# Attention with few key-value heads and an MLP: row maxima by pairs, with a difference product on ScalarE

## The chip, the cores and the metric

The kernel runs on one core of a Trainium2 chip. The metric is the device time of one execution in microseconds, the median of several runs; lower is better. The engines are PE (TensorE: products), ACT (ScalarE), DVE (VectorE), POOL (GpSimd) and SP (SyncE, which issues the transfers). Sums of products go to PSUM, in eight banks of 128 x 512 numbers; ScalarE and VectorE read them there.

## The reference

The computation is one transformer block on x (1 x 2048 x 512) with 32 query heads of 16 numbers each, all on one head of keys and values, and an MLP of 1376 hidden numbers. Six vectors from c and w_mod shift, scale and gate the two halves.

```python
h = _layernorm(x, axis=-1) * (1 + ca) + sa
q = (h @ wq).reshape(B, S, H, Dh)          # 32 heads of 16
k = h @ wk                                 # one head
v = h @ wv
scores = jnp.einsum("bhqd,bkd->bhqk", q, k) * (Dh ** -0.5)
p = softmax(scores); o = p @ v
x = x + ga * (o @ wo)
h = _layernorm(x, axis=-1) * (1 + cb) + sb
x = x + gb * (gelu(h @ w1 + b1) @ w2 + b2)
```

The softmax subtracts each row's maximum over all 2048 keys. That maximum is what the change is about: it takes one product of queries with keys only to find it, and a second one for the scores that are exponentiated.

## The kernel before, in words

Numbers are kept at fp32 accuracy by splitting operands into a high and a low part (`split`, L128), so that most products come in threes.

**Prologue** (L1241 to L1302, some 75 us): the first normalization, keys (`ks`, L109: 64 rows for each half of the array), values (`va`), and the first queries. Tiles that only the prologue needs are in the pool `pro`.

**Main loop** (L1350 to L1448). The queries are cut into 8 blocks of 256 rows, a block into 8 units of 4 heads: 64 units. A unit runs in 4 passes of the loop, a pass in two *half cycles*. A half cycle issues, in an order that `issue` (L1320) and `mixture` (L1330) write out from lists:

- four maximum products `m` (`Max.step`, L498 to L506): 128 queries by 512 keys, each on one half of the array (s = 0 or 1). Each goes to one of three banks (tag "m"), and VectorE reduces it to a column of `mx` (L510). The list of a side (L488) goes along the four key blocks kc of a row of queries. When a unit's list is through, `put_max` (L529) joins the columns and writes the maxima into the queries' tile, so that the score product subtracts them.
- four score products `e` of a later unit (`sexp`, L590 to L607) into three banks in turn (L586), each followed by the exponential on ScalarE into a tile p (L611). There are three p tiles of four slots.
- a batch of *filling products* of other work, where the queue has one (`take`, L1169): late query projections (qps, L448), output projection (wops, L864), turns of the normalized rows (tp, L928), the MLP's two matrices (w1ps, L990, and w2ps, L1022). The two sides of the array take half of each.
- at its end 16 products `acc` of p and values for an earlier step (`pv`, L617 to L628, each of two passes, of which the trace has one record each).

Each engine has its own queue and takes it in the order in which the program issues (L214). In the loop there are three forms of half cycles. `short` (L1395) is a batch of at most four products' worth of 512 columns: six with 256 columns at the start of w1ps, three left over at the start of w2ps, four turns, four late query products. Their order is (first half; the second has the sides exchanged):

```python
issue(mixture(maxes(1, n // 2), exps(1, [(X, 0), (X, 1)])),
      exps(0, [(X, 0)]) + halves(batch, 0) + [(1.0, lambda: follow(0, X, 1))])
```

Larger batches have an order of their own (L1400 and L1430). Without a batch, `plain` (L1381) takes two maximum products of each side, and one of them gets the bank "x" as its fourth. `issue` takes from the list that has got less far, the first list on a tie.

Behind the loop the last block's rest runs by itself ("fast", L821 to L825 load its weight pieces into the free p tiles). A queue of jobs (`put_off`, L1166) decides which filling work comes when; clocks (`later`, L145) count half steps, not time. Copies out of PSUM in that work are on ScalarE at L454 (late queries in small batches) and L895 (turned rows).

Of the kernel before, what the change touches and what calls it, by code (L numbers as in the profile page):

```python
# [18 lines left out]

GELU_R = 0.044715 ** 0.5  # L20

LEAD = 6
# [23 lines left out]
def raw(ap):  # L46
    return ap.bitcast(F32)
# [3 lines left out]
def adaln_mqa_mlp(  # L51
# [199 lines left out]
    load_x(1)  # L251
    nc.sync.dma_start(out=wqf[:, :, P:2 * P], in_=wqr[:, :, P:2 * P])
    load_x(2)
    nc.sync.dma_start(out=wqf[:, :, 2 * P:D], in_=wqr[:, :, 2 * P:D])
    load_x(3)
    qbufs = [att.tile([P, 2, HQ], F32R, name=f"qst{i}") for i in range(QBUFS)]

    qbufs = [att.tile([P, 2, HQ], F32R, name=f"qst{i}") for i in range(QBUFS)]
# [47 lines left out]

    pad(pro, 64, "pad2")
    wkH = pro.tile([P, KD, P], F32R, name="wkH")
# [171 lines left out]
    class Max:  # L480


        def __init__(self):
            def products(u, kcs):
                return [(u, j, t, kc) for kc in kcs for j in range(2) for t in range(blocks[units[u][0]][1] // P)]

            def in_rows(u):
                return [(u, j, t, kc) for j in range(2) for t in range(blocks[units[u][0]][1] // P) for kc in range(NKC)]  # L488


            begin = [o for u, kc in FIRST_MAX for o in products(u, [kc])]
            self.todo = [begin + [o for u in range(2, NU) for o in in_rows(u)] for _ in range(2)]
            self.mx, self.left, self.done = {}, list(size), 0

        def has(self, s):
            return bool(self.todo[s])

        def step(self, s, hold=None, **place):  # L498
            u, j, t, kc = self.todo[s].pop(0)
            T = blocks[units[u][0]][1] // P  # L500
            if u not in self.mx:
                self.mx[u] = att.tile([P, 4 * T, NKC], F32, name=f"mx{u}", tag="mx", bufs=2)
            m = psum.tile([P, 512], F32, name=f"m{u}_{j}_{t}_{kc}_{s}", **(place or dict(tag="m", bufs=3)))
            rows = slice(64 * s, 64 * s + 64)
            nc.tensor.matmul(m, qsts[u][rows, j, t * P:(t + 1) * P], ks[rows, kc * 512:(kc + 1) * 512],  # L505
                             start=True, stop=True)  # L506
            i = (s * 2 + j) * T + t

            def reduce():
                nc.vector.tensor_reduce(out=self.mx[u][:, i, kc:kc + 1], in_=m, axis=AX.X, op=ALU.max)  # L510
                self.left[u] -= 1
                if self.left[u] == size[u] // 2 and u > 1 and u + 1 < NU:
                    load_q(u + 1)
                if self.left[u] == 0:
# [14 lines left out]
    def put_max(u, mx):  # L529
# [36 lines left out]
        else:  # L566
            later((0 - clock[0]) % 4 + 1, reduce)

    pbufs = {}
    ocs = []  # L570
# [19 lines left out]
    def sexp(u, K, j, s, line=None):  # L590

        w = blocks[units[u][0]][1]
        qst = qsts[u]
        assert u in placed
        n = u * steps[0] + K
        if n < 3 and n not in pbufs:
            pbufs[n] = att.tile([P, 2, 2, 512], F32, name=f"p{n}", tag="p", bufs=3)
        pt = pbufs[n % 3]
# [4 lines left out]
        if w == 512:  # L603
            kt, rhs = K, qst[rows, j, :]
        else:
            kt, rhs = 2 * K + j, qst[rows].rearrange("p j n -> p (j n)")
        nc.tensor.matmul(e, ks[rows, kt * P:(kt + 1) * P], rhs, start=True, stop=True)  # L607
        dst = pt[:, j, s, :]

        def exp():  # L610
            ins = nc.scalar.activation(dst, e, AF.Exp, scale=0.25)  # L611
            for old in written.pop((n - 3, j, s), ()):
                tc.declare_no_dep(ins.ins, old, reason="the products that read the tile's last contents come between the two")
            written.setdefault((n, j, s), []).append(ins.ins.name)
            return ins

        return exp() if line is None else line.append(exp)  # L617

    def pv(u, K):
        w = blocks[units[u][0]][1]  # L620
        if K == 0:
            accs[u] = psum.tile([P, w], F32, name=f"acc{u}", tag="v")
        pt = pbufs[(u * steps[0] + K) % 3]
        for kt in ([K] if w == 512 else [2 * K, 2 * K + 1]):
            for cidx in range(4):
                s, j = divmod(cidx, 2)
                rhs = pt[:, j, s, :] if w == 512 else pt[:, kt - 2 * K, s, j * w:(j + 1) * w]
                ins = nc.tensor.matmul(accs[u][32 * cidx:32 * cidx + 32, :], va[:, kt, :], rhs,  # L628
                                       start=kt == 0, stop=kt == NKT - 1)
                if kt % 2 and cidx:  # L630
                    wait_early(ins)

    def finish_unit(u):
# [174 lines left out]
    def rest_steps(b, fast, rp, bank, ons, ready):  # L808
# [4 lines left out]
        for hf in range(w // HQ):  # L813
# [7 lines left out]
            if fast:  # L821
                for f in range(3, 9, 2):
                    two = att.tile([P, 2, 2, KD, P], F32R, name=f"w1t{b}_{hf}_{f}", tag="p", bufs=3)
# [68 lines left out]
            def modulate(dp, ps):  # L892
                if not fast:
                    src = rp.tile([P, 2, HQ], F32, name=f"tc{b}_{hf}_{dp}", tag="ot", bufs=2)
                    nc.scalar.copy(src, ps)  # L895
                for d2 in range(2):
# [453 lines left out]
    for u in range(NU):  # L1350
        for K in range(0, steps[u], 2):
# [59 lines left out]
            if batch:  # L1411
# [88 lines left out]
```

## Time and profile before

| | before |
|---|---|
| time of the runs, median of three | 1564.88 us (1564.7 to 1564.99) |
| span of the profiled execution, first to last instruction | 1563.1 us |
| VectorE: maximum reduces | 2048, mean 682 ns |
| ScalarE: exponentials | 2048, mean 598 ns |
| granted TensorE clock | 1.000 |

The profiled execution has no time of its own in the record beside its span; the runs' median is 1.8 us above it. In the profile's lines, `L510 DVE TENSOR_REDUCE mx<-m ... x2048 | 1270.5, 682` means: line 510, on VectorE, writes mx from m, 2048 times, 1270.5 us in which at least one was under way, 682 ns each on average; then the idle time before them and what ended it. Neighbours overlap, so that the time from one start to the next is shorter than the duration. In the view in order of time a row is start, duration, engine, line, operation, tiles and count; neighbours of one form are merged.

### The profile page before, as it was taken

Reading aid. Unit: us, or ns where it says so; the run is one execution under the profiler, and the core shown is the slowest. Engines: PE = TensorE matmul, PEld = TensorE weight load, DVE = VectorE, ACT = ScalarE, POOL = GpSimd, SP = SyncE. Lnnn points to the kernel's source line nnn. Section 1 sums busy time; section 2 is a strip of 40 time slices with the busy share of each in tenths; the row PEclk is TensorE's granted clock in tenths of the full one; section 3 lists DMA queues with packets and bytes.
Section 4 is the critical chain, followed back from the end, with each engine's and each line's share of the span. In section 5 each row is a group of like instructions: output and inputs, shape, how many; then the busy total and the mean of one; then the engine's idle time right before and its main releaser. Section 6 shows DMA issues by size and latency. Waiting matters only on the chain.

```text
span 1563.1 us, 41433 instructions
## 1 busy us (share of the span) xinstructions
PE 1546.5 (99%) x16387; PEld 959.9 (61%) x16387; DVE 1401.7 (90%) x2479; ACT 1228.8 (79%) x2392; POOL 681.7 (44%) x1194
## 2 busy tenths in 40 slices
PE   7999999999999999999999999999999999999999
PEld 4455555567655665557655675556655676556667
DVE  7999999999999999999999999999999999999625
ACT  5577778788777887788877887788877888788853
POOL 5545433877323570246422472245611573235711
PEclk9999999999999999999999999999999999999999
DMA  7235412313030211213022120303112130312241
GB/s 244 97 96 194 152 52 89 120 52 97 19 110 19 83 60 35 93 29 99 29 62 69 57 84 26 105 16 97 43 50 79 46 97 20 102 34 66 81 150 61
DMA packets 83126, 121.63 MB, mean 78 GB/s; under 512 B 19614, under 2 KB 56222, under 8 KB 82676
## 3 DMA queue, kind: packets, MB, share of 16 engines
q1 hardware_dynamic: 82916, 118.97, 23.5%
q8 instruction: 130, 2.13, 0.6%
q14 instruction: 64, 0.52, 0.1%
q10 hardware_dynamic: 16, 0.00, 0.0%
HBM read 91.13 MB, written 27.27 MB: 76 GB/s over the span
## 4 chain that ended last, share of the span: by engine, by line
PE 84%; DVE 10%; issue 3%; POOL 2%; DMA 1%; ACT 0%; ACTq 0%; SPq 0%; POOLq 0%; DVEq 0%
PE acc L628 28%; PE m L505 24%; PE e L607 16%; DVE mx L510 8%; PE w1ps L191 8%; PE w2ps L181 2%; PE w2ps L191 1%; PE w1ps L181 1%; DMA xt<-in_A_x_dram 1%; PE qps L191 1%; PE tp L191 1%; PE wops L191 1%; PE kps L162 1%; DVE st L835 1%; DVE x L828 1%
## 5 line engine op out<-in xcount | busy, mean ns | idle before, releaser
L510 DVE TENSOR_REDUCE mx<-m 128x1 f32<-128x512 f32 x2048 | 1270.5, 682 | 86.9 <-PE m L505 63.8
L611 ACT ACTIVATE p<-e 128x512 f32<-128x512 f32 x2048 | 1099.3, 598 | 257.4 <-PE e L607 110.5
L505 PE MATMUL m<-ks,qst 64*128 64x512 f32 x2048 | 832.4, 429 | 1.9 <-DVE mx L510 0.6
L607 PE MATMUL e<-qst,ks 64*128 64x512 f32 x2048 | 747.6, 412 | 0.1
L628 PE MATMUL acc<-p,va 128*32 128x256 f32 x8192 | 548.0, 385 | 0.0
L505 PEld LDWEIGHTS m<-ks,qst 64*128 64x128 f32 x2048 | 366.5, 184 | 212.3 <-DVE mx L510 174.8
L607 PEld LDWEIGHTS e<-qst,ks 64*128 64x128 f32 x2048 | 362.5, 184 | 95.2 <-ACT p L611 71.1
L628 PEld LDWEIGHTS acc<-p,va 128*32 128x32 f32 x8192 | 213.7, 109 | 213.1 <-issue 110.0
L553 POOL TENSOR_SCALAR mt<-turned 8x32 f32<-8x32 f32 x256 | 53.1, 208 | 418.9 <-DVE turned L559 406.9
L191 PE MATMUL w1ps<-h2H,w1t 64*128 64x256 f32 x1232 | 235.6, 287 | 0.0
L191 PEld LDWEIGHTS w1ps<-h2H,w1t 64*128 64x128 f32 x1232 | 185.8, 184 | 28.9 <-DVE mx L510 17.7
L191 PE MATMUL w1ps<-h2L,w1t 64*128 64x256 f32 x616 | 169.2, 275 | 0.0
L191 PE MATMUL w2ps<-w2H,gH 64*128 64x512 f32 x284 | 123.8, 436 | 0.0
L191 PEld LDWEIGHTS w1ps<-h2L,w1t 64*128 64x128 f32 x616 | 114.0, 185 | 0.0
L191 PE MATMUL w2ps<-w2L,gH 64*128 64x512 f32 x282 | 110.9, 393 | 0.0
L191 PE MATMUL w2ps<-w2H,gL 64*128 64x512 f32 x282 | 110.2, 391 | 0.0
L954 POOL TENSOR_SCALAR tt<-tt 128x256 f32<-128x256 f32 x77 | 31.0, 403 | 142.6 <-ACT tt L953 109.3
L137 POOL TENSOR_TENSOR gL<-z,gH 128x256 fp32r<-128x256 f32 x77 | 57.0, 740 | 6.4
L955 POOL TENSOR_TENSOR tt<-tt,z 128x256 f32<-128x256 f32 x77 | 56.7, 736 | 6.4
L965 POOL TENSOR_TENSOR z<-tt,z 128x256 f32<-128x256 f32 x77 | 56.4, 733 | 6.0
L964 POOL TENSOR_TENSOR tt<-tt,z 128x256 f32<-128x256 f32 x77 | 56.4, 732 | 0.0
L191 PEld LDWEIGHTS w2ps<-w2H,gL 64*128 64x128 f32 x282 | 52.2, 185 | 0.4
(190 smaller groups left out, 1480.9 us busy)
## 6 DMA issues: line engine op xcount, KB each, us to landing
w1t<-dw SPq DMA_DIRECT2D x82, 512.0 KB
qst<-dq SPq DMA_DIRECT2D x384, 32.0 KB
do<-oc SPq DMA_DIRECT2D x64, 128.0 KB
dw<-w1s SPq DMA_DIRECT2D x11, 512.0 KB
xt<-in_A_x_dram SPq DMA_DIRECT2D x4, 1024.0 KB
dq<-qH SPq DMA_DIRECT2D x16, 256.0 KB
dq<-qL SPq DMA_DIRECT2D x16, 256.0 KB
x<-in_A_x_dram SPq DMA_DIRECT2D x8, 512.0 KB
```

Of the source, the lines that this page charges most:

```text
L137: eng_l.tensor_tensor(out=dst_l, in0=src, in1=raw(dst_h), op=ALU.subtract)
L181: nc.tensor.matmul(ps, a, b_, start=first_, stop=last_)
L191: ins = nc.tensor.matmul(ps, a[rows], b_[rows], start=first_ and s == 0, stop=last_ and s == 1)
L505: nc.tensor.matmul(m, qsts[u][rows, j, t * P:(t + 1) * P], ks[rows, kc * 512:(kc + 1) * 512], start=True, stop=True)
L510: nc.vector.tensor_reduce(out=self.mx[u][:, i, kc:kc + 1], in_=m, axis=AX.X, op=ALU.max)
L553: nc.gpsimd.tensor_scalar(out=mt[:, g:g + 32], in0=turned[g:g + 4 * T, :], scalar1=1.0, scalar2=0.0, op0=ALU.mult, op1=ALU.add)
L607: nc.tensor.matmul(e, ks[rows, kt * P:(kt + 1) * P], rhs, start=True, stop=True)
L611: ins = nc.scalar.activation(dst, e, AF.Exp, scale=0.25)
L628: ins = nc.tensor.matmul(accs[u][32 * cidx:32 * cidx + 32, :], va[:, kt, :], rhs, start=kt == 0, stop=kt == NKT - 1)
L955: nc.gpsimd.tensor_tensor(out=tt, in0=tt, in1=z, op=ALU.mult)
L964: nc.gpsimd.tensor_tensor(out=tt, in0=tt, in1=z, op=ALU.mult)
L965: nc.gpsimd.tensor_tensor(out=z, in0=tt, in1=z, op=ALU.add)
```

## The change

Two maxima over neighbouring key blocks a and b are joined: max(a, b) = b + max(a - b, 0). Once in the loop, `differences` makes `kd`, the differences of the key blocks 0 - 1 and 2 - 3. Then a product of queries with kd takes the place of the product with the even block; ScalarE takes its positive part (`ramp`), and VectorE adds the odd block's product and reduces the sum to its maximum in one operation (`tensor_tensor_reduce`), instead of two reduces. This is done for the first two products of one side in the half cycles without a batch (`plain`) and in the short ones; half cycles with larger batches stay as they are. As only one column of two is written then, the columns are filled with the lowest number beforehand.

To make room for `kd` and two tiles of positive parts, the exponentials get eight slots in two p tiles instead of twelve in three. Tiles of the prologue and of the last block that used the third p tile get other places. The copies of L454 and L895 go from ScalarE to VectorE.

```diff
+    kd = const.tile([P, NKC // 2, 512], F32R, name="kd", tag="kd")
...
-        xt = att.tile([P, QT, D], F32, name=f"xt{b}", tag="p", bufs=3)
+        xt = pro.tile([P, QT, D], F32, name=f"xt{b}", tag="xp") if b == 2 else att.tile([P, QT, D], F32, name=f"xt{b}", tag="p", bufs=2)
...
-              [att.tile([P, 4, D], F32, name=f"wml{k}", tag="p", bufs=3)])
+              [pro.tile([P, 4, D], F32, name=f"wml{k}", tag="xp") if k == 3 else att.tile([P, 4, D], F32, name=f"wml{k}", tag="p", bufs=2)])
...
+    rs_ = att.tile([P, 2, 512], F32, name="ramps", tag="ramps")
...
-        if size_ == SHORT:
-            nc.scalar.copy(q32, ps)
-        else:
-            nc.vector.tensor_copy(out=q32, in_=ps)
+        nc.vector.tensor_copy(out=q32, in_=ps)
...
+        def columns(self, u):
+            if u not in self.mx:
+                T = blocks[units[u][0]][1] // P
+                self.mx[u] = att.tile([P, 4 * T, NKC], F32, name=f"mx{u}", tag="mx", bufs=2)
+                if u > 1:
+                    nc.gpsimd.memset(self.mx[u], LOWEST)
+
+        def pair(self, s):
+
+            two = self.todo[s][:2]
+            return bool(kds) and len(two) == 2 and two[0][3] % 2 == 0 and two[1] == (*two[0][:3], two[0][3] + 1)
+
+        def ramp(self, s):
+
+            u, j, t, kc = self.todo[s].pop(0)
+            m = psum.tile([P, 512], F32, name=f"m{u}_{j}_{t}_{kc}_{s}", tag="m", bufs=3)
+            rows = slice(64 * s, 64 * s + 64)
+            nc.tensor.matmul(m, qsts[u][rows, j, t * P:(t + 1) * P], kd[rows, kc // 2, :], start=True, stop=True)
+            r = rs_[:, self.beside % 2, :]
+            self.beside += 1
+            nc.scalar.activation(r, m, AF.Relu)
+            self.ramps[s] = r
+            self.done += 1
...
-                nc.vector.tensor_reduce(out=self.mx[u][:, i, kc:kc + 1], in_=m, axis=AX.X, op=ALU.max)
+                if r is None:
+                    nc.vector.tensor_reduce(out=self.mx[u][:, i, kc:kc + 1], in_=m, axis=AX.X, op=ALU.max)
+                else:
+                    nc.vector.tensor_tensor_reduce(out=r, in0=m, in1=r, scale=1.0, scalar=LOWEST, op0=ALU.add, op1=ALU.max,
+                                                   accum_out=self.mx[u][:, i, kc:kc + 1])
+                    self.left[u] -= 1
...
+    def differences():
+
+        both = wts_pool["rest"].tile([P, 2, P], F32R, name="both", tag="h322", bufs=2)
+        nc.gpsimd.memset(raw(both), 0.0)
...
+        yield 4
+        for i in range(NKC // 2):
+            ps = psum.tile([P, BQ], F32, name=f"kdps{i}", tag="x")
+            yield [(ps, both[:, n, :], ks[:, (2 * i + n) * 512:(2 * i + n + 1) * 512], n == 0, n == 1) for n in range(2)]
+            nc.scalar.copy(kd[:, i, :], ps)
+            nc.vector.tensor_tensor(out=kd[32:48, i, :], in0=ps[32:48, :], in1=raw(kd[32:48, i, :]), op=ALU.subtract)
+            nc.scalar.copy(kd[96:112, i, :], raw(kd[32:48, i, :]))
+        kds.append(True)
+
+    free = list(range(8))
...
-            pbufs[n] = att.tile([P, 2, 2, 512], F32, name=f"p{n}", tag="p", bufs=3)
+            pbufs[i // 4] = att.tile([P, 4, 512], F32, name=f"p{i // 4}", tag="p", bufs=2)
...
-                for f in range(3, 9, 2):
+                for f in range(3, 7, 2):
...
+                for f, (pool_, tag) in ((7, (const, "kd")), (8, (att, "ramps"))):
+                    w1ts[f] = pool_.tile([P, 2, KD, P], F32R, name=f"w1t{b}_{hf}_{f}", tag=tag)
+                    nc.sync.dma_start(out=raw(w1ts[f]), in_=dw1[f])
...
-                    nc.scalar.copy(src, ps)
+                    nc.vector.tensor_copy(out=src, in_=ps)
...
-    put_off(*late, late_mods(), *[qproj_late(b, g) for b in range(2, NB) for g in range(KD)])
+    put_off(differences(), *late, late_mods(), *[qproj_late(b, g) for b in range(2, NB) for g in range(KD)])
...
+            def first_pair(s, n, held=None):
+
+                todo = maxes(s, n, held=held)
+                if n > 1 and mp.pair(s):
+                    todo[0] = 1.0, lambda: mp.ramp(s)
+                return todo
...
-                one, other = maxes(s, n), maxes(t, n)
+                one, other = first_pair(s, n), maxes(t, n)
...
-                issue(mixture(maxes(1, n // 2), exps(1, [(X, 0), (X, 1)])),
+                issue(mixture(first_pair(1, n // 2), exps(1, [(X, 0), (X, 1)])),
...
-                    issue(mixture(maxes(0, n // 2, held=hold), exps(0, [(Y, 0), (Y, 1)])),
+                    issue(mixture(first_pair(0, n // 2, hold), exps(0, [(Y, 0), (Y, 1)])),
```

More of the change, by code (lines that the diff above doesn't have):

```diff
@@ L20 @@
 GELU_R = 0.044715 ** 0.5
+LOWEST = -3.4028234663852886e38
 LEAD = 6
@@ L252, in adaln_mqa_mlp @@
     nc.sync.dma_start(out=wqf[:, :, P:2 * P], in_=wqr[:, :, P:2 * P])
+    pad(pro, 32, "pad9")
     load_x(2)
@@ L255, in adaln_mqa_mlp @@
     load_x(3)
-    qbufs = [att.tile([P, 2, HQ], F32R, name=f"qst{i}") for i in range(QBUFS)]
+    rs_ = att.tile([P, 2, 512], F32, name="ramps", tag="ramps")
     qbufs = [att.tile([P, 2, HQ], F32R, name=f"qst{i}") for i in range(QBUFS)]
@@ L500, in step @@
             T = blocks[units[u][0]][1] // P
-            if u not in self.mx:
-                self.mx[u] = att.tile([P, 4 * T, NKC], F32, name=f"mx{u}", tag="mx", bufs=2)
+            self.columns(u)
             m = psum.tile([P, 512], F32, name=f"m{u}_{j}_{t}_{kc}_{s}", **(place or dict(tag="m", bufs=3)))
@@ L507, in step @@
             i = (s * 2 + j) * T + t
+            r, self.ramps[s] = self.ramps[s], None
             def reduce():
-                nc.vector.tensor_reduce(out=self.mx[u][:, i, kc:kc + 1], in_=m, axis=AX.X, op=ALU.max)
+                if r is None:
[4 more added lines that the diff above has]
+                    self.left[u] -= 1
+                before_ = self.left[u] + (r is not None)
                 self.left[u] -= 1
-                if self.left[u] == size[u] // 2 and u > 1 and u + 1 < NU:
+                if self.left[u] <= size[u] // 2 < before_ and u > 1 and u + 1 < NU:
                     load_q(u + 1)
+                    self.columns(u + 1)
                 if self.left[u] == 0:
@@ L567, in put_max @@
             later((0 - clock[0]) % 4 + 1, reduce)
+    kds = []
+    def differences():
+        both = wts_pool["rest"].tile([P, 2, P], F32R, name="both", tag="h322", bufs=2)
+        nc.gpsimd.memset(raw(both), 0.0)
+        for r in (0, 32):
+            for o in (0, 64):
+                nc.gpsimd.tensor_scalar(out=both[r:r + 16, 0, o:o + 48].rearrange("p (r n) -> p r n", n=16),
+                                        in0=ident[r:r + 16, r:r + 16].unsqueeze(1).to_broadcast([16, 3, 16]),
+                                        scalar1=1.0, scalar2=0.0, op0=ALU.mult, op1=ALU.add)
+        nc.gpsimd.tensor_scalar(out=both[:, 1, :], in0=raw(both[:, 0, :]), scalar1=-1.0, scalar2=0.0, op0=ALU.mult, op1=ALU.add)
+        yield 4
[7 more added lines that the diff above has]
+    free = list(range(8))
+    slots = {}
     pbufs = {}
@@ L590, in sexp @@
     def sexp(u, K, j, s, line=None):
-        w = blocks[units[u][0]][1]
         qst = qsts[u]
         assert u in placed
-        n = u * steps[0] + K
-        if n < 3 and n not in pbufs:
-            pbufs[n] = att.tile([P, 2, 2, 512], F32, name=f"p{n}", tag="p", bufs=3)
-        pt = pbufs[n % 3]
+        i = slots[u, K, j, s] = free.pop(0)
+        if i // 4 not in pbufs:
+            pbufs[i // 4] = att.tile([P, 4, 512], F32, name=f"p{i // 4}", tag="p", bufs=2)
         bank = banks.pop(0)
@@ L602, in sexp @@
         rows = slice(64 * s, 64 * s + 64)
[L603 to L606, printed above, removed]
+        kt, rhs = 2 * K + j, qst[rows].rearrange("p j n -> p (j n)")
         nc.tensor.matmul(e, ks[rows, kt * P:(kt + 1) * P], rhs, start=True, stop=True)
-        dst = pt[:, j, s, :]
+        dst = pbufs[i // 4][:, i % 4, :]
         def exp():
             ins = nc.scalar.activation(dst, e, AF.Exp, scale=0.25)
-            for old in written.pop((n - 3, j, s), ()):
-                tc.declare_no_dep(ins.ins, old, reason="the products that read the tile's last contents come between the two")
-            written.setdefault((n, j, s), []).append(ins.ins.name)
+            if i in written:
+                tc.declare_no_dep(ins.ins, written[i], reason="the products that read the tile's last contents come between the two")
+            written[i] = ins.ins.name
             return ins
@@ L622, in pv @@
             accs[u] = psum.tile([P, w], F32, name=f"acc{u}", tag="v")
-        pt = pbufs[(u * steps[0] + K) % 3]
-        for kt in ([K] if w == 512 else [2 * K, 2 * K + 1]):
+        for kt in (2 * K, 2 * K + 1):
             for cidx in range(4):
                 s, j = divmod(cidx, 2)
-                rhs = pt[:, j, s, :] if w == 512 else pt[:, kt - 2 * K, s, j * w:(j + 1) * w]
+                i = slots[u, K, kt - 2 * K, s]
+                rhs = pbufs[i // 4][:, i % 4, j * w:(j + 1) * w]
                 ins = nc.tensor.matmul(accs[u][32 * cidx:32 * cidx + 32, :], va[:, kt, :], rhs,
@@ L631, in pv @@
                     wait_early(ins)
+            free.extend(slots.pop((u, K, kt - 2 * K, s)) for s in range(2))
     def finish_unit(u):
@@ L821, in rest_steps @@
             if fast:
-                for f in range(3, 9, 2):
-                    two = att.tile([P, 2, 2, KD, P], F32R, name=f"w1t{b}_{hf}_{f}", tag="p", bufs=3)
+                for f in range(3, 7, 2):
+                    two = att.tile([P, 2, 2, KD, P], F32R, name=f"w1t{b}_{hf}_{f}", tag="p", bufs=2)
                     nc.sync.dma_start(out=raw(two), in_=dw1[f:f + 2].rearrange("f p i k n -> p f i k n"))
                     w1ts[f], w1ts[f + 1] = two[:, 0], two[:, 1]
+                for f, (pool_, tag) in ((7, (const, "kd")), (8, (att, "ramps"))):
+                    w1ts[f] = pool_.tile([P, 2, KD, P], F32R, name=f"w1t{b}_{hf}_{f}", tag=tag)
+                    nc.sync.dma_start(out=raw(w1ts[f]), in_=dw1[f])
             def add_x(t, ps):
```

3 lines of the change are left out of this document (2 added, 1 removed).

## The prediction

> **What bounds the kernel now.** I read the page first: shares, the chain that ended last, the costliest groups.
>
> ```profile
> span 1563.1 us, 41433 instructions
> PE 1546.5 (99%) x16387; PEld 959.9 (61%) x16387; DVE 1401.7 (90%) x2479; ACT 1228.8 (79%) x2392; POOL 681.7 (44%) x1194
> PE 84%; DVE 10%; issue 3%; POOL 2%; DMA 1%; ACT 0%; ACTq 0%; SPq 0%; POOLq 0%; DVEq 0%
> L510 DVE TENSOR_REDUCE mx<-m 128x1 f32<-128x512 f32 x2048 | 1270.5, 682 | 86.9 <-PE m L505 63.8
> L611 ACT ACTIVATE p<-e 128x512 f32<-128x512 f32 x2048 | 1099.3, 598 | 257.4 <-PE e L607 110.5
> ```
>
> VectorE is 90% busy, ScalarE 79%, so moving work from the first to the second looks right. But shares are averages, and the chain runs through PE. So I cut the loop into half cycles. Each ends with the acc products (L628, 16 records), so acc records divided by 16 count the halves of any stretch. By the lines of the filling products there are three kinds. In the views by windows, for the acc records alone, the first column behind the window is its length. Full halves (5 or 6 products' worth, which the change leaves alone), one stretch of several:
>
> ```profile
> 436.30:487.50 51.20, 19.27 (x288) 7.51 (x288) 0.74 (x2) 1.00 0.27 84
> ```
>
> That is 18 halves at 2.84 us. Short halves (at most four products' worth: late queries, turns, the first third of w1ps, the start of w2ps), twenty windows, first, one of the middle, last:
>
> ```profile
> 204.20:253.39 49.19, 19.27 (x288) 7.51 (x288) 0.74 (x2) 1.00 0.15 52
> ...
> 498.02:519.83 21.81, 8.56 (x128) 3.33 (x128) 0.37 (x1) 1.00 0.06 17
> ...
> 1398.17:1419.97 21.80, 8.56 (x129) 3.34 (x129) 0.37 (x1) 1.00 0.08 22
> sum 267.83, PE 104.92 PEld 40.88 ACT 5.58; mean PE 5.25 PEld 2.04 ACT 0.28
> ```
>
> The first holds 18 halves, seven like the middle one hold 8 each, and twelve of w2ps hold 2 each: 98 halves, 2.73 us each. (Two more come behind the last reduce and stay out.) Empty halves, eight windows:
>
> ```profile
> 253.39:284.73 31.34, 12.85 (x193) 5.02 (x193) 0.74 (x2) 1.00 0.36 111
> ...
> 1387.56:1398.17 10.61, 4.28 (x65) 1.67 (x65) 0.00 (x0) 1.00 0.14 37
> sum 105.04, PE 42.83 PEld 16.70 ACT 0.74; mean PE 5.35 PEld 2.09 ACT 0.09
> ```
>
> 12 halves and seven times 4: 40 halves, 2.63 us each. Now what ends a half. One empty half in order of time, ScalarE and then PE:
>
> ```profile
> 491.65 2.06 ACT L611 ACTIVATE p<-e 128x512 f32<-128x512 f32 x4 [0.55 <-PE e L607]
> ```
> ```profile
> 491.11 0.51 PE L607 MATMUL e<-qst,ks 64*128 64x512 f32 x2
> 491.45 0.40 PE L505 MATMUL m<-ks,qst 64*128 64x512 f32 x2
> 491.69 0.39 PE L607 MATMUL e<-qst,ks 64*128 64x512 f32 x1
> 491.69 0.86 PE L505 MATMUL m<-ks,qst 64*128 64x512 f32 x2
> 492.30 0.50 PE L607 MATMUL e<-qst,ks 64*128 64x512 f32 x1
> 492.73 1.07 PE L628 MATMUL acc<-p,va 128*32 128x256 f32 x16
> 493.73 0.51 PE L607 MATMUL e<-qst,ks 64*128 64x512 f32 x2
> ```
>
> Four score products e go through three banks, so the fourth takes the bank of the first. The first exponential starts 0.54 us after its product (491.11, 491.65), lasts 0.60, and 0.05 later the fourth product starts (492.30). 0.43 later come the acc products, and 1.00 later the next half: 0.54 + 0.60 + 0.05 + 0.43 + 1.00 = 2.62. **This loop is latency**: ScalarE is free for 0.55 us of it, but not at the point where it counts. A short half:
>
> ```profile
> 333.30 1.58 ACT L611 ACTIVATE p<-e 128x512 f32<-128x512 f32 x3 [0.65 <-PE e L607]
> ```
> ```profile
> 333.27 1.89 DVE L510 TENSOR_REDUCE mx<-m 128x1 f32<-128x512 f32 x3 [0.23 <-PE e L607]
> ```
> ```profile
> 331.73 1.07 PE L628 MATMUL acc<-p,va 128*32 128x256 f32 x16
> 332.73 0.50 PE L505 MATMUL m<-ks,qst 64*128 64x512 f32 x1
> 332.74 0.72 PE L607 MATMUL e<-qst,ks 64*128 64x512 f32 x2
> ...
> 334.02 0.50 PE L607 MATMUL e<-qst,ks 64*128 64x512 f32 x1
> 334.45 0.42 PE L628 MATMUL acc<-p,va 128*32 128x256 f32 x4
> ```
>
> Here all four maximum products m share three banks too (an empty half gives one of them a fourth bank). The fourth waits for the first reduce: 333.27 + 0.68 + 0.06 = 334.01, and the fourth e stands behind it on PE. Without it that e could have gone at 333.30 + 0.60 + 0.05 = 333.95. So VectorE costs a short half some 0.07 to 0.1 us against an empty one, no more. That such a delay goes one to one into the half shows where a transpose held the first reduce back by some 0.2 us:
>
> ```profile
> 238.69 1.84 DVE L510 TENSOR_REDUCE mx<-m 128x1 f32<-128x512 f32 x3
> ```
> ```profile
> 236.92 1.07 PE L628 MATMUL acc<-p,va 128*32 128x256 f32 x16
> 237.92 0.50 PE L505 MATMUL m<-ks,qst 64*128 64x512 f32 x1
> ...
> 239.40 0.50 PE L607 MATMUL e<-qst,ks 64*128 64x512 f32 x1
> 239.82 0.42 PE L628 MATMUL acc<-p,va 128*32 128x256 f32 x4
> ```
>
> The reduce starts 0.77 us into the half instead of 0.54, the fourth e at 1.48 instead of 1.29, and the half takes 2.90 instead of 2.72.
>
> **The change, part by part.** Each pair removes one reduce of VectorE. Its price is its spacing, (1.89 - 0.68) / 2 = 0.60 us. It adds one activation of the same shape on ScalarE at (1.58 - 0.60) / 2 = 0.49. The number of products stays.
>
> *Short halves.* The written order decides. In `issue` the first group begins with the new product, so its positive part is issued on ScalarE before all four exponentials. The new product starts with the half, as m does now, and its activation can start where the reduce starts now, at 0.54. Behind it in ScalarE's queue waits the first exponential (0.54 + 0.49 = 1.03, until now 0.57). The fourth e waits for that one, and the acc products wait for that e: 1.03 + 0.60 + 0.05 = 1.68, + 0.43 + 1.00 = **3.11 us**. The fourth m no longer matters, as its bank comes free with the activation at 1.14. So 98 × 3.11 = 304.8 against 267.83: **+37.0 us**. What made some of them longer until now (late reduces, up to 2.90) is covered by the new wait.
>
> *The added function's spacing* has no row. The nearest are those of the exponential (0.49) and of a copy of the same shape, 0.61 long:
>
> ```profile
> L895 ACT COPY tc<-tp x14: 607/607/608, 323.8 to 1409.4; 128x512 f32<-128x512 f32 x14
> ```
>
> I take 0.49. The ends are 0.46, if it overlapped its neighbours somewhat more, and 0.61, with no overlap: 98 × (-0.03 to +0.12) = -3 to +12 us. The Trainium skill (ScalarE: Activation LUTs, section "What ACT_TABLE_LOAD costs") gives every function the same rate: 186 ns + 0.833 ns per element, less 93 ns between neighbours. By that the spacing is an estimated 520 ns and the term some 3 us larger; the trace's 0.49 for the exponential is below it, and I keep the trace's.
>
> *Empty halves.* Here the order is two exponentials, the positive part, two exponentials. The first is not delayed, so the loop keeps 2.62. ScalarE now has 5 × 0.49 = 2.45 in it: the third exponential ends near 2.6 and the fourth near 3.1 after the start, just before the next half's first can begin (2.62 + 0.54 = 3.16). The cover is thin: a copy of acc (0.37, the ACT column of the windows above, one in eight halves) goes over it by some 0.2, for about 5 of these halves: +1.0. Two of the old 40 lose a late reduce: 36 × 2.61 = 94.0, and the other four become short halves without a pair (below), 4 × 2.71 = 10.8; together 104.8 against 105.04: -0.2.
>
> *The combined operation* of VectorE (sum, maximum) is in no row. From below, a reduce of the shape spaces at 0.60; from above, I allow twice that, 1.2. A short half then needs 1.2 + 2 × 0.6 = 2.4 of VectorE in 3.11, an empty one 2.4 in 2.62, so either end is covered: 0. It starts only after the activation, at about 1.2 in a short half; behind it wait two reduces, whose banks the next half needs at 3.11 + 0.57 and later: in time.
>
> *The differences of keys*: two batches of two products take four half cycles early (counted above). At the end of each, ScalarE copies, VectorE subtracts, ScalarE copies again, all ahead of an exponential: it comes some 0.6 + 0.7 + 0.6 late, of which about 1.1 us reaches the next half: 2 × 1.1 = +2.2. The rest of the queue moves by two cycles into the twelve empty halves at 253 us, which cover it.
>
> *Moved and small*: 3 + 14 copies go from ScalarE to VectorE, about a reduce's 0.6 us each, into short halves where VectorE drops one reduce; the two held reduces behind such a copy free their banks within the longer half: 0. A clearing of mx on GpSimd per unit is queued half a unit, four halves or 11 us, ahead of need: 0; were GpSimd further behind than that, a unit's first reduce would wait. The p slots go from 12 to 8; an exponential then reuses what the acc products just ahead of its own score product have read, which PE's order already ensures: 0. On SP's queue, one tile of x and one of modulations get another tile with the same order, and the tail's last weight load of two pieces becomes two loads: 0, within 1 us.
>
> **Sum**: 37.0 + 1.0 - 0.2 + 2.2 = +40.0, made against this execution: 1603.1 of span. The median of the runs is 1.8 above this span (1564.88 to 1563.1), so the forecast is **1605 us**.
>
> **Rivals.** (1) *No more overlap on ScalarE between unlike functions*: 0.61 at the two seams of the activation. Short halves 3.23: 98 × 3.23 = 316.5, +48.7; an empty half then needs 3 × 0.49 + 2 × 0.61 = 2.69 of ScalarE: 36 × 0.07 = +2.5; with 1.0 + 2.2 - 0.2: 1564.9 + 54 = 1619. For it: nothing tells how this function follows an exponential. Against: copies behind exponentials in this trace leave no gap. (2) *Faster*: the activation does not hold the first exponential, because the fourth e is not what the half waits for, and only VectorE's relief counts. The short halves fall to the 2.61 of empty ones: 98 × 2.61 = 255.8, -12, with +3 from the rest 1556. It decides from the point where the activation's delay of the first exponential falls under 0.1 us. For it: VectorE is the later of the two in short halves now. Against: ScalarE takes its queue in order. The larger gain that the busy shares suggest, 134 × 0.60 = 80 us, would need VectorE as the bound of these halves, and an empty half, 2.63 against its loop's 2.62, hardly waits for it. (3) *It doesn't do what it says*: few pairs form, as they need an even key block in front at each half. 1564.9 + 0.4 + 2.2 = 1567. Against: all three kinds of halves take four products, two or four of a side. (4) *A table load* around each activation:
>
> ```profile
> 0.72 1.28 ACT L270 ACT_TABLE_LOAD   x1 [0.72 <-PEq L1486]
> ```
>
> 134 × 2 × 1.28 = 343: 1950. Against: this is the trace's only one, though tanh, square and exp alternate. The Trainium skill (ScalarE: Activation LUTs, "Table sets: the hidden batching unit") has relu in every set, which speaks against it as well; no run here shows it yet.
>
> **How the numbers follow.** The forecast 0.77, (1) 0.08, (2) 0.10, (3) 0.04, (4) 0.01. The forecast's own range: 1605 - 3 (0.46 spacing) - 2.2 - 1 - 2 (full halves that gain a little) = 1597, and up to 1605 + 12 with the unlapped spacing, 1617. Reaching to (1), 1597 to 1620 holds about 8 in 10. Faster by over 0.2% (3 us, about what a measurement of this kernel can tell from no change): 0.10, from (2). Within: 0.04, from (3). Slower: 0.86.
>
> **What would show it.** Right: short halves near 3.11 us, the activation as the first of five on ScalarE, the fourth e some 1.68 after the start with PE's wait put down to ScalarE; full halves still 2.84, empty ones 2.6; VectorE's share down to near 85%. Wrong: the first exponential still at 0.57 (order not as read), short halves under 2.71 (rival 2), empty halves over 2.7 (rival 1), fewer than 120 combined operations (rival 3), further table loads (rival 4).

## The result, and the profile after

| | before | after |
|---|---|---|
| median of the runs | 1564.93 us (1564.7 to 1567.52, 4 runs) | 1605.39 us (1604.74 to 1606.49, 4 runs) |
| span of the profiled execution | 1563.1 us | 1603.0 us |

The ratio is 1.0256, 95% interval 1.0241 to 1.027: slower, 0.4 us from the forecast of 1605.

The page of the kernel after: shares, then the shares of the chain, then the groups of maximum reduces and combined operations; the last line, of the positive parts, is from the view by lines.

```profile
span 1603.0 us, 41812 instructions
PE 1578.7 (98%) x16395; PEld 971.5 (61%) x16395; DVE 1340.2 (84%) x2498; ACT 1289.0 (80%) x2513; POOL 689.9 (43%) x1263
...
PE 94%; ACT 3%; POOL 1%; DMA 1%; DVE 1%; issue 0%; SPq 0%; DVEq 0%; POOLq 0%
...
L535 DVE TENSOR_REDUCE mx<-m 128x1 f32<-128x512 f32 x1780 | 1113.9, 683 | 93.5 <-PE m L528 85.4
...
L537 DVE CUSTOM_DVE_ANT_0 ramps<-m,ramps 128x512 f32<-128x512 f32 x134 | 92.6, 691 | 93.9 <-ACT ramps L518 83.2
...
L518 ACT ACTIVATE ramps<-m 128x512 f32<-128x512 f32 x134 | 80.5, 601 | 35.5 <-PE e L656 34.6
```

The change does what it says: 268 reduces have become 134 pairs, VectorE's share falls from 90% to 84%, its 10% of the chain shrinks to 1%. ScalarE, which had 0% of the chain, now has 3% of it. The time still grew. Where, the same cut into half cycles shows (the 16 acc records that end a half are eight products in the code, with two records each): the windows of the kernel after for the acc records, the short halves with a pair (the first of twenty windows and the sum), then the sum of the eight windows of empty halves, then the four halves that make the differences.

```profile
217.85:273.55 55.70, 19.27 (x289) 7.51 (x289) 0.75 (x2) 1.00 0.16 52
...
sum 303.45, PE 104.94 PEld 40.91 ACT 5.60; mean PE 5.25 PEld 2.05 ACT 0.28
```
```profile
sum 94.02, PE 38.53 PEld 15.01 ACT 0.42; mean PE 4.82 PEld 1.88 ACT 0.05
```
```profile
90.38:102.70 12.32, 4.28 (x64) 1.67 (x65) 0.37 (x1) 1.00 0.37 107
```

The 98 short halves went from 267.83 to 303.45 us, 2.73 to 3.096 each: **+35.6 of the 39.9 us**. The empty ones are 36 × 2.612 (before 40 × 2.626). With the four of the differences the former empty stretches grew from 105.04 to 106.34, +1.3.

One short half of the kernel after in order of time, ScalarE, VectorE and PE (left out are the filling products, one m and one e):

```profile
718.74 0.60 ACT L518 ACTIVATE ramps<-m 128x512 f32<-128x512 f32 x1 [0.54 <-PE e L656]
719.24 2.06 ACT L660 ACTIVATE p<-e 128x512 f32<-128x512 f32 x4
```
```profile
719.38 0.69 DVE L537 CUSTOM_DVE_ANT_0 ramps<-m,ramps 128x512 f32<-128x512 f32 x1 [1.19 <-ACT ramps L518]
719.99 0.09 DVE L537 DVE_READ_ACCUMULATOR2_ANT mx<- 128x1 f32 x1
```
```profile
718.21 0.49 PE L515 MATMUL m<-kd,qst 64*128 64x512 f32 x1
718.22 0.72 PE L656 MATMUL e<-qst,ks 64*128 64x512 f32 x2
...
719.25 0.65 PE L528 MATMUL m<-ks,qst 64*128 64x512 f32 x2
719.88 0.49 PE L656 MATMUL e<-qst,ks 64*128 64x512 f32 x1
720.30 1.07 PE L677 MATMUL acc<-p,va 128*32 128x256 f32 x16
```

The half starts at 718.21. The positive part starts 0.53 later, the first exponential 0.50 after that (719.24), lasts 0.60, and the fourth e starts 0.04 behind its end (719.88, 1.67 into the half). The acc products follow 0.42 later and last 1.00. VectorE waited 1.19 us in front of the combined operation: the engine that was relieved stands idle.

### The profile page after: what moved, and what is told of

It reads as the page before. It is cut to its first block, busy times and chain, and to the rows that moved or that the text cites. A ratio compares the mean times of both kernels' runs of the same rounds, so it can differ in the third digit from the quotient of the medians.

```text
span 1603.0 us, 41812 instructions
## 1 busy us (share of the span) xinstructions
PE 1578.7 (98%) x16395; PEld 971.5 (61%) x16395; DVE 1340.2 (84%) x2498; ACT 1289.0 (80%) x2513; POOL 689.9 (43%) x1263
## 4 chain that ended last, share of the span: by engine, by line
PE 94%; ACT 3%; POOL 1%; DMA 1%; DVE 1%; issue 0%; SPq 0%; DVEq 0%; POOLq 0%
PE acc L677 32%; PE m L528 22%; PE e L656 20%; PE w1ps L193 7%; PE m L515 3%; PE w2ps L193 2%; PE w2ps L183 2%; PE qps L193 1%; PE wops L193 1%; ACT p L660 1%; PE w1ps L183 1%; DMA xt<-in_A_x_dram 1%; ACT ramps L518 1%; PE tp L193 1%; PE kps L164 1%; PE wops L183 0%
## 5 line engine op out<-in xcount | busy, mean ns | idle before, releaser
L660 ACT ACTIVATE p<-e 128x512 f32<-128x512 f32 x2048 | 1101.3, 599 | 202.0 <-PE e L656 64.2
L535 DVE TENSOR_REDUCE mx<-m 128x1 f32<-128x512 f32 x1780 | 1113.9, 683 | 93.5 <-PE m L528 85.4
L528 PE MATMUL m<-ks,qst 64*128 64x512 f32 x1914 | 772.6, 422 | 1.4 <-DVE mx L535 0.8
L656 PE MATMUL e<-qst,ks 64*128 64x512 f32 x2048 | 752.0, 413 | 8.1 <-ACT p L660 6.3
L677 PE MATMUL acc<-p,va 128*32 128x256 f32 x8192 | 548.0, 385 | 0.0
L656 PEld LDWEIGHTS e<-qst,ks 64*128 64x128 f32 x2048 | 364.0, 184 | 138.4 <-ACT p L660 116.1
L528 PEld LDWEIGHTS m<-ks,qst 64*128 64x128 f32 x1914 | 346.1, 184 | 154.5 <-DVE mx L535 117.8
L677 PEld LDWEIGHTS acc<-p,va 128*32 128x32 f32 x8192 | 213.7, 109 | 212.9 <-issue 113.5
L537 DVE CUSTOM_DVE_ANT_0 ramps<-m,ramps 128x512 f32<-128x512 f32 x134 | 92.6, 691 | 93.9 <-ACT ramps L518 83.2
L518 ACT ACTIVATE ramps<-m 128x512 f32<-128x512 f32 x134 | 80.5, 601 | 35.5 <-PE e L656 34.6
L515 PE MATMUL m<-kd,qst 64*128 64x512 f32 x134 | 62.5, 467 | 0.0
L1008 POOL TENSOR_TENSOR tt<-tt,z 128x256 f32<-128x256 f32 x77 | 57.0, 740 | 6.4
```

What stands on the lines that cost most here:

```text
L515: nc.tensor.matmul(m, qsts[u][rows, j, t * P:(t + 1) * P], kd[rows, kc // 2, :], start=True, stop=True)
L518: nc.scalar.activation(r, m, AF.Relu)
L537: nc.vector.tensor_tensor_reduce(out=r, in0=m, in1=r, scale=1.0, scalar=LOWEST, op0=ALU.add, op1=ALU.max, accum_out=self.mx[u][:, i, kc:kc ...
L1008: nc.gpsimd.tensor_tensor(out=tt, in0=tt, in1=z, op=ALU.mult)
```

## The experiments

**Theory:** a short half is a loop through ScalarE: first exponential, bank of the fourth e, acc products. The positive part delays the first exponential by its own spacing, and that goes one to one into the half. **Rivals:** the price is ScalarE's extra load, wherever it stands; it is VectorE's combined operation; or it comes from the moved copies and tiles. Line numbers differ by a few from kernel to kernel: the products e are at L656 to L659, the exponential at L660 to L663, the acc products at L677 to L685.

### The suspected step doubled: e6_twice

```diff
             nc.scalar.activation(r, m, AF.Relu)
+            if twice:
+                nc.scalar.activation(r, m, AF.Relu)
...
```

(`twice` is true in short halves only.) The positive part is taken two times from the same product.

> Edit: in short halves the positive part is taken twice from the same product into the same tile, both ahead of the exponentials; the result is the same. Theory: another 0.49 on the way to the fourth e in each of 98 halves, 3.09 becomes 3.58 (up to 3.75 if the second waits for the first one's end): 1605.4 + 48 = 1653, up to 1670 us. Rival (half of the loss is the wait for the bank or the combined operation on VectorE, not the activation's own time): clearly less than 1640 us.

Measured: 1665.13 us, ratio 1.0644 (1.0629 to 1.066), in the upper part of the expected range. A short half on ScalarE (it starts at 745.92), and the sum of the windows of all 98:

```profile
746.45 0.60 ACT L518 ACTIVATE ramps<-m 128x512 f32<-128x512 f32 x1 [0.54 <-PE e L658]
747.08 0.60 ACT L520 ACTIVATE ramps<-m 128x512 f32<-128x512 f32 x1
747.57 1.57 ACT L662 ACTIVATE p<-e 128x512 f32<-128x512 f32 x3
```
```profile
sum 365.47, PE 104.93 PEld 40.90 ACT 5.59; mean PE 5.25 PEld 2.05 ACT 0.28
```

Short halves take 3.73 us, 0.63 more than after. The second positive part starts 0.63 behind the first (0.49 was expected, 0.64 allowed for), so the delay of the first exponential goes one to one into the half, 98 times: 365.47 - 303.45 = 62.0 us. The medians differ by 59.7, because a loss of some 2.6 us outside the short halves, described below, does not occur here. That the step lies on the loop is shown.

### The same load without the wait: e5_nowait

No differences and no pairs; instead each short half issues first, on ScalarE, a positive part of a tile in SBUF that is always ready. Its result is not used.

```diff
...
+                        nc.scalar.activation(rs_[:, 1, :], rs_[:, 0, :], AF.Relu)
+                        step_()
...
```

> Edit: the kernel without pairs, with one more activation of 128x512 in each short half, at the place of the positive part (ahead of all four exponentials), but from one SBUF tile to another, so that it waits for no product; its result is not used. Theory (what costs is that the activation waits for its product and then stands before the first exponential; ScalarE itself is idle for 0.55 to 0.65 us ahead of it): it runs while the acc products do and is out of the way, so 1568.5 plus 0 to 8 us. Rival (a fifth operation on ScalarE costs its 0.49 wherever it starts): 98 x 0.4, some 1608 us.

Measured: 1573.41 us, ratio 1.006 (1.0042 to 1.0077); against its own base e4_none (below) +5.0. A short half, ScalarE and PE:

```profile
699.69 0.66 ACT L1425 ACTIVATE ramps<-ramps 128x512 f32<-128x512 f32 x1
700.48 1.58 ACT L661 ACTIVATE p<-e 128x512 f32<-128x512 f32 x3
```
```profile
699.91 0.50 PE L529 MATMUL m<-ks,qst 64*128 64x512 f32 x1
...
701.19 0.50 PE L657 MATMUL e<-qst,ks 64*128 64x512 f32 x1
```

The half starts at 699.91. The extra activation starts 0.22 us *before* that, while the acc products of the half before are under way. The first exponential starts at 0.57 and the fourth e at 1.28, as in the kernel before the change; the half is 2.71 long. So ScalarE's load is not the price: an activation of the same shape, here from SBUF, costs nearly nothing (0.9 us in the 74 short halves outside of w2ps, against e4_none) in the 0.5 us in which ScalarE waits for the first score product anyway. What costs is that the positive part waits for a product of its own half, and the first exponential waits in the queue behind it. Most of the 5 us (3.9) are in the 24 short halves of w2ps, where the tanh of the MLP is queued between the exponentials too; what makes it dearer there was not tried.

### The positive part behind the first exponential: e1_second

```diff
-            nc.scalar.activation(r, m, AF.Relu)
             self.ramps[s] = r
+            behind_one.append(lambda: nc.scalar.activation(r, m, AF.Relu))
...
```

In short halves the list is run right behind the issue of the next exponential. The order on PE is unchanged.

> Edit: in short halves the positive part is issued on ScalarE behind the first exponential instead of ahead of all four; the difference product stays the first maximum product on PE. Theory (the fourth e and the fourth m are both waited for by the acc products, each through a bank that its first product holds): the first exponential is back at 0.57 us, so the fourth e could go at 1.22; but the positive part now starts at 0.57 + 0.49 = 1.06 and ends at 1.66, only then is its bank free for the fourth m, which PE takes ahead of the fourth e: 1.66 + 0.06 = 1.72, so the half takes 1.72 + 1.43 = 3.15, no gain: 1605 to 1611 us. Rival (only the delay of the first exponential counts): short halves fall to 2.71, 1605.4 - 98 x 0.38 = 1568 us.

Measured: 1611.31 us, ratio 1.0298 (1.0282 to 1.0313), 0.3 above the expected range. A short half (starts at 722.25):

```profile
722.82 0.60 ACT L663 ACTIVATE p<-e 128x512 f32<-128x512 f32 x1 [0.58 <-PE e L659]
723.31 0.59 ACT L519 ACTIVATE ramps<-m 128x512 f32<-128x512 f32 x1
```
```profile
722.25 0.50 PE L515 MATMUL m<-kd,qst 64*128 64x512 f32 x1
...
723.96 0.50 PE L530 MATMUL m<-ks,qst 64*128 64x512 f32 x1 [0.28 <-ACT ramps L519]
723.96 0.49 PE L659 MATMUL e<-qst,ks 64*128 64x512 f32 x1
```

The first exponential is at 0.57 again, and nothing is won: now the fourth *m* waits for the bank that the positive part reads until 723.90, and the fourth e stands behind it on PE (723.96 = 1.71 into the half). Two loops run through ScalarE, one by the banks of e and one by the banks of m, and whichever operation comes second delays a fourth product. As long as the pair is first on PE, neither of the two orders tried on ScalarE saves it. Of the 5.9 us that this kernel takes more than after, 3.8 lie in the 98 short halves and 1.3 in the wait on SP described below.

### The pair in the middle: e2_middle and e10_not_w2

```diff
...
+                a, b_, c_, d = mp.todo[s][:4]
+                mp.todo[s][:4] = [c_, a, d, b_]
+                todo = maxes(s, n, held=held)
+                todo[1] = 1.0, lambda: mp.ramp(s)
...
```

The four maximum products of a short half come as plain, difference, plain, and the product of the sum last. The first bank is then freed by an ordinary reduce, and the positive part is issued behind two exponentials.

> Edit: in short halves the four maximum products go in the order single, difference, single, sum, so that the positive part comes third on ScalarE, behind two exponentials, and the first bank is freed by a reduce of VectorE as before the change. Theory (loop through the banks): first exponential at 0.57, fourth e free at 1.22, fourth m at 0.54 + 0.68 + 0.06 = 1.28: short halves 2.71, 98 x 2.71 = 265.6 instead of 303.4: 1567.6 us, between 1564 and 1571. Rival (a fifth operation on ScalarE costs its 0.49 wherever it stands): still 1605 us. Second rival (VectorE as the bound, one reduce of 0.6 fewer in 98 halves): under 1560 us.

Measured: 1579.82 us, ratio 1.0096 (1.0081 to 1.0111): missed by 12. The windows of its 98 short halves:

```profile
sum 269.72, PE 104.92 PEld 40.89 ACT 6.13; mean PE 5.25 PEld 2.04 ACT 0.31
```

269.72 against 303.45: **the loss in short halves is gone**, 33.7 of 35.6 us, with as many pairs (134) and combined operations as before the edit. So neither the combined operation nor a fifth operation on ScalarE is the price by itself. Of the 12 us missed, 4.1 lie in these halves, which take 2.75 and not the expected 2.71. The rest lies outside of them. Twelve full halves, the first of w2ps behind its short halves, took 3.28 to 3.39 instead of 2.84. One of them, ScalarE and PE:

```profile
591.99 0.64 ACT L518 ACTIVATE ramps<-m 128x512 f32<-128x512 f32 x1
592.46 1.15 ACT L660 ACTIVATE p<-e 128x512 f32<-128x512 f32 x2
```
```profile
593.15 0.50 PE L528 MATMUL m<-ks,qst 64*128 64x512 f32 x1
593.75 0.47 PE L193 MATMUL w2ps<-w2H,gH 64*128 64x512 f32 x1
593.76 0.50 PE L656 MATMUL e<-qst,ks 64*128 64x512 f32 x1
```

The half starts at 593.15, but its first filling product and the first e behind it come only at 593.75, 0.14 after the last exponential of the half before (592.46 + 1.15 = 593.61). In the code the filling products of a large batch are placed behind an exponential by a wait. With a positive part ahead of it that exponential is late. As a test, e10_not_w2 is e2_middle with plain maxima in the short halves of w2ps alone:

```diff
-                issue(mixture(middle_pair(1, n // 2), exps(1, [(X, 0), (X, 1)])),
+                issue(mixture((maxes if len(batch) == 3 else middle_pair)(1, n // 2), exps(1, [(X, 0), (X, 1)])),
...
```

> As e2_middle, but the 24 short halves with three w2ps products take plain maxima instead of the middle pair. If the 5.9 us that e2's twelve following w2ps halves lost come from the late last exponential of such a short half, they go: 1579.8 - 5.9 - 0.5 (those 24 halves at 2.72 again) = 1573.4, within 1.5. Rival: those halves were late for another reason (the second column of the pair, the differences ahead of them), and the time stays within 1 of 1579.3.

Measured: 1574.94 us, ratio 1.0057 (1.004 to 1.0074), 4.9 below e2 and 1.5 above the expectation. The sum of the windows of the twelve full halves, in e2_middle and then in e10_not_w2:

```profile
sum 40.03, PE 12.84; mean PE 1.07
```
```profile
sum 34.27, PE 12.86; mean PE 1.07
```

40.03 to 34.27, -5.8: that the pairs in the short halves ahead of them are the cause is shown; that they act through the late exponential is read from the rows above and the code. Of the 10 us that e10 still loses, some 2 lie in its short halves and 2.5 with the differences; the largest part is one long half near 344 us and the one behind it, which e2 has too. SP and PE of e2_middle there:

```profile
326.50 18.12 SPq L1182 DMA_DIRECT2D w2f<-in_B_w_dram  x2
```
```profile
348.48 0.49 PE L656 MATMUL e<-qst,ks 64*128 64x512 f32 x1 [3.35 <-DMA qst<-ml]
```

A weight load stands 18 us on SP's queue, and behind it the transfers that bring the next unit's maxima (qst) to PE. That half takes 7.4 us in e2 and 7.9 in e10, 4.5 to 5 over the usual 2.85; with the half behind it the loss is 5.3 in e2 and 6.1 in e10. The kernel after has the same in a smaller measure (below). And even without these the middle place would gain nothing: its short halves (269.72) are no shorter than those before (267.83), although VectorE has one reduce less in each.

### The parts one by one: e3_empty, e4_none, e9_layout, e7_copies, e8_late

e3_empty has pairs in empty halves alone:

```diff
-                issue(mixture(first_pair(1, n // 2), exps(1, [(X, 0), (X, 1)])),
+                issue(mixture(maxes(1, n // 2), exps(1, [(X, 0), (X, 1)])),
...
```

> Edit: pairs in empty halves alone; the short ones take four plain reduces again; all else as in the changed kernel. Theory: all of the loss but some 4 us lies in the 98 short halves: back from 303.4 to 267.8, so 1605.4 - 35.6 = 1569.8 us, between 1567 and 1572, with empty halves still 2.61. Rival (the extra activation loads ScalarE in every kind of half): a good part of the loss stays, over 1580 us.

Measured: 1575.62 us, ratio 1.007 (1.0055 to 1.0085): 5.8 above the expectation. Two things make this up. The short halves take 3.5 us more than in the kernel before, as they now have the moved copies without the longer half that covered them. And one half takes 7.7 us with the wait on SP: with the one behind it it loses 5.3, where the kernel after, from which the expectation was reckoned, loses 2.6.

e4_none has no differences and so no pairs; all that the change moves stays:

```diff
-    put_off(differences(), *late, late_mods(), *[qproj_late(b, g) for b in range(2, NB) for g in range(KD)])
+    put_off(*late, late_mods(), *[qproj_late(b, g) for b in range(2, NB) for g in range(KD)])
```

> Edit: no differences of keys and no pairs; the eight slots, the clearing of mx, the moved tiles and the two copies on VectorE stay. Theory: these cost nothing, 1565 us within 1.5 of the kernel before. Rival (fewer slots or the moved copies hold the loop): over 1568 us. With the run that has pairs in empty halves it also gives the price of the differences with those pairs: some 2 to 4 us.

Measured: 1568.45 us, ratio 1.0026 (1.0016 to 1.0036), 2 above the expected range. In a half with a turn, VectorE and PE show why:

```profile
505.34 0.68 DVE L948 COPY tc<-tp 128x512 f32<-128x512 f32 x1
505.94 3.67 DVE L535 TENSOR_REDUCE mx<-m 128x1 f32<-128x512 f32 x6
```
```profile
506.31 0.50 PE L528 MATMUL m<-ks,qst 64*128 64x512 f32 x1
...
507.87 0.50 PE L528 MATMUL m<-ks,qst 64*128 64x512 f32 x1
```

The copy pushes the reduces back, the fourth m starts 1.56 us into the half (506.31 to 507.87) instead of 1.28, and the half takes 2.99. e9_layout is e4_none with the two copies back on ScalarE, e7_copies the whole change with them back:

```diff
-                    nc.vector.tensor_copy(out=src, in_=ps)
+                    nc.scalar.copy(src, ps)
...
```

> Edit: no differences, no pairs, and the copies of the late queries and of the turned rows back on ScalarE; what stays of the change are the eight slots for exponentials, the clearing of mx and the moved tiles. Theory (without pairs the copies on VectorE hold reduces back and made the 3.7 us of the run that kept them there; the rest costs nothing): 1564.7 within 1 us. Rival (the slots or the clearing cost it): still 1567 us or more.

> Edit: the changed kernel with the copies of the late queries and of the turned rows back on ScalarE. Theory: beside pairs these copies are hidden on either engine, 1605 us within 2. Rival (they hold VectorE's reduces with the pairs too, as they do without pairs, where moving them and the other small parts cost 3.7 us): some 3 us less, 1602 us.

Measured: e9 1564.95 us, ratio 1.000 (0.9991 to 1.0009); e7 1605.96 us, ratio 1.0263 (1.0248 to 1.0278). So the 3.5 us of e4 are the copies; the new places of the tiles, the eight p slots and the clearing of mx cost nothing that shows; and with the pairs in place the copies cost nothing either: the longer half covers them.

e8_late is the whole change with the differences at the end of the early queue (`put_off(*late, ..., differences())`), to see what their place costs.

> Edit: the differences of keys are made after the late queries instead of before them. Theory (their two cycles delay all later work of the queue; SP then stands longer at a load of w2 that waits for GpSimd, with the transfers of the maxima behind it, which makes one half of 4.9 us at 353 us): that half is back near 2.85, but the 18 short halves of the late queries lose their pairs (18 x 0.37 = 6.7), and the differences then come late themselves: 1605.4 - 2.6 - 6.7 = 1596 us, between 1594 and 1599. Rival (the long half has another cause, such as the clearing of mx): the half stays long, 1599 us or more.

Measured: 1598.26 us, ratio 1.0219 (1.0202 to 1.0236), as expected, 7 below after. The long half near 353 us is gone. The differences do not become free: their four halves take 13.13 us there, against 12.32.

## Why the prediction was right, and where its steps were off

**Short halves (+37.0, measured +35.6).** The mechanism held in each link: 0.53 + 0.50 + 0.60 + 0.04 = 1.67 for the fourth e, + 0.42 + 1.00 = 3.09. It was 0.015 per half too large, from links rounded up. e6 and e5 show that the delayed first exponential is the price, and not ScalarE's load. The waits say the same. The kernel after, from the view of waits, those of PE's weight loads by what ended them (sum in us, how many, the longest in us), for m, for the new product and for e:

```profile
PEld m L528 <- DVE mx L535: 117.8, 284, 0.8
PEld m L515 <- DVE mx L535: 28.0, 68, 0.4
PEld e L656 <- ACT p L660: 116.1, 432, 0.7
```

Before:

```profile
PEld m L505 <- DVE mx L510: 174.8, 441, 0.8
PEld e L607 <- ACT p L611: 71.1, 316, 0.4
```

The wait for reduces fell from 174.8 to 145.8 us, the wait for exponentials rose from 71.1 to 116.1. VectorE's relief is real, but the wait moved to ScalarE.

**Spacing of the added function (0.49).** It is 0.50 in the half shown and 0.49 in the mean of all 134, as long as an exponential's. The estimate of 520 ns worked out from the Trainium skill (ScalarE: Activation LUTs, "What ACT_TABLE_LOAD costs") is a little above the trace here too.

**Empty halves (-0.2 and +1.0).** The 36 with a pair take 94.02 against the 94.0 reckoned. The overflow by copies of acc (+1.0) does not show: this term was too large by all of it.

**Combined operation (0.6 to 1.2, taken as covered).** Its spacing is 0.61 (719.38 to 719.99), that of a reduce, and in a short half VectorE idles in front of it.

**Differences (+2.2).** Their four halves take 12.32 against 10.84, and the full half behind them 4.03 against 2.84, of which the kind as a whole shows +1.0: together +2.5. The size was right. But the sentence that the rest of the queue moves into the empty halves, **"which cover it", failed**. The kernel after, SP and PE:

```profile
332.81 19.01 SPq L1182 DMA_DIRECT2D w2f<-in_B_w_dram  x2
351.91 0.65 SPq L579 DMA_DIRECT2D qst<-mh  x1
```
```profile
355.67 0.47 PE L656 MATMUL e<-qst,ks 64*128 64x512 f32 x1 [1.72 <-DMA qst<-ml]
```

Two halves take 4.90 and 3.40 instead of 2.85: +2.6, a term that the sum does not have. Before, the same load stood 11.47 us at 300.95 and nobody waited. The view of the waits on SP's queue puts 18.3 of the 19.01 us down to GpSimd (before, 10.7 of 11.47). With the differences at the end of the queue (e8), or without them (e4, e5, e9), no such half occurs. With them in front it occurs in after, e1, e2, e3, e7 and e10, but not in e6. There the load stands even longer, 20.87 us, but the transfers behind it start 4.2 us ahead of the half that needs them (365.60 and 369.76), in after only 1.6 us (351.91 and 353.46). So with the differences in front the load stands longer (e8, with them at the end: 11.50 us), and what that costs depends on when the transfers behind it are needed. A run with nothing but the load freed was not tried.

**The sum (+40.0, measured +39.9).** The main term was right by its mechanism. That the total was met to 0.1 us is luck: the loss just described, which was not foreseen, and the two terms that came out too large, short halves (1.4) and copies of acc (1.0), cancel.

**Moved and small (0).** e9 and e7 agree. The moved copies are free only under the longer half, as was said; without it they cost 3.5 us (e4 against e9).

**Rivals.** (1) fell: no seam of the positive part with an exponential behind it or ahead of it is longer than 0.50. (2) fell: a short half without the delay (e2) is 2.75, not 2.61. (3) fell: 134 pairs, 98 + 36. (4) fell: the trace after has one table load as well.

```profile
L272 ACT ACT_TABLE_LOAD x1 | 1.3, 1283 | 0.7 <-PEq L1546 0.7
```

No version tried beats the kernel before; e9 equals it.

## What to carry to other kernels

The busiest engine after the bound need not be the one to relieve. Write down the loop of one stage, instruction by instruction, and ask which start moves: here 134 × 0.6 us of VectorE's work went away and gained nothing, and one activation ahead of the first exponential cost its whole spacing each time. In this kernel an operation added to an engine's queue was cheap when its input was ready before the engine's idle stretch (e5), or, within its own half, when it stood behind what the loop waits for (e2), and dear when it had to wait itself. A job put in front of a queue also shifts what comes behind it, transfers among them: look at the queue of the engine that issues them too.

## What the runs showed that was not expected

- The combined operation leaves two records: 691 ns, and 83 ns for the read of the accumulator. The next reduce starts at the same moment as the second (719.99), so it costs no spacing here.
- A positive part right behind another that writes the same tile from the same bank starts 0.63 us after it (e6); behind it an exponential of another bank follows after 0.49. Whether the tile or the bank makes the difference was not tried.
- In e1, issuing the positive part later made the half longer (3.14 against 3.10): with the pair first, the loop by the banks of m is as tight as that by the banks of e.
